# Gated linear attention in front of a token mixer: the attention rebuilt on 64-token blocks

## The chip, the core and the metric

The kernel runs on one core of one Trainium2 chip. The metric is the device time of one execution in microseconds, read as the median of several runs. The engines are named as in the profile: PE multiplies matrices (PEld loads its stationary side), DVE, ACT and POOL are the elementwise engines, and SP issues the DMA transfers.

## The reference

Four batches with eight heads of width 40 run over 768 tokens. Each head carries a 40x40 state C and a normalizer n; both fade by the forget gate and grow by the input gate, with a running maximum m that keeps the exponentials small:

```python
m_new  = np.maximum(f_gate[:, :, t] + m, i_gate[:, :, t])
f_stab = np.exp(f_gate[:, :, t] + m - m_new)
i_stab = np.exp(i_gate[:, :, t] - m_new)
C = f_stab * C + i_stab * outer(v_t, k_t);   n = f_stab * n + i_stab * k_t
h_t = sigmoid(o_gate_t) * (C @ q_t) / max(|n . q_t|, 1)
```

The heads are put side by side to rows x of width 320, and the mixer follows: theta = x @ w_theta, zr = x cos(theta), zi = x sin(theta), y = w_tok_r @ zr + w_tok_i @ zi over the tokens, u = x + y, and the output u + relu(u @ w_ch). The three weight matrices arrive as 64-bit floating point, handed over as integers, and the kernel turns each into a sum of two 32-bit parts; a mixer product is then three products of parts.

## The kernel before

The work is cut into 24 attention tasks, n = 4c + b for chunk c (six chunks of 128 tokens) and batch b, and 12 mixers, q = 2c + pr, one for two batches. A task loads q and k transposed (`qk`), and k and v by token (`tok`). The matrix E of decays, 128 x 8 x 128, comes in chunk 0 from four PE products (`assemble`, L292) and in the later chunks from a broadcast load of cumulated gates out of DRAM (L425), on which ACT takes an exponential with one bias per head (L430, eight a task). POOL clears what is not causal (L436). PE makes the scores `sc` from 64-row halves, two heads at a time (L445), DVE multiplies them by E (L449), and PE sums, per head, the scores times the values, into the single-bank tile `ph` (L464). Behind chunk 0 the state is read into the same sums: queries scaled by the decay (`qs`, L453) against C, three heads in one product of 120 rows (L461). From `ph` DVE takes the denominator (L474, L475), the output gate (L480) and the output X (L486). For the next chunk the keys are faded (L500), PE makes the state's growth `st` (L506), the old state is faded (`wane`, L510) and DVE adds the growth (`up`, L519). One state a chunk is carried, for 128 tokens.

A mixer transposes X (L542), splits it into two parts (L544, L545), makes the angles (L557, L563), rounds them to whole turns, takes sine and cosine on ACT (L582, L583), multiplies by X (`zm`, L588) and splits again (`zh`, `zl`, L589, L590). Five groups of twelve products (L601) mix the tokens of a chunk into all 768, and DVE adds each group to the accumulator `acc` (L616; for chunk 0, L608 to L612). The weights of a chunk come in two pieces, each turned into two parts by `split`: size (`_abs`), two exponent steps (`_up`, L343 and L344), sign (L347), low bits (L350), rounding (L358) and remainder (L359). At the end `channel` splits u and makes the channel products (L671, L681), DVE adds the relu (L691) and SP stores.

PSUM holds three tiles of two banks (`two`) and two of one bank (`one`). Nothing is scheduled at run time: every step is a task with the engines that may do it, and the string `ORDER` lists number and engine (T for PE, V, A, G, D for a DMA issue on SP) of each in the order of issue. Each engine works its part of this list in order; a tile's slot goes round in the same order.

Of the kernel before, what the change touches and what calls it, by code (L numbers as in the profile page):

```python
# [8 lines left out]
F32 = mybir.dt.float32  # L9
# [8 lines left out]
DM = H * D  # L18
# [4 lines left out]
KD = 3 * D  # L23
TOK = 9 * D + H * E1
# [4 lines left out]
HEAD = [3 * g + j for j in range(3) for g in range(3) if 3 * g + j < H]  # L29
RANK = [HEAD.index(h) for h in range(H)]  # L30
SPREAD = (0,)
# [4 lines left out]
LEAST = 2.0**-15  # L36
WCOLS = 1792

ORDER = """
4V 24T 0D 1D 2V 60V 62V 63V 3A 108D 67A 70D 61G 64V 68V 69G 65A 109V 82D 66V 71A 74D 83A 141D 124D 143T 145A 126T 111V  # L40
144A 84V 112V 148T 113V 72D 110G 131T 142D 125D 127A 114V 128A 75A 209T 147G 85V 116V 115D 129G 86V 73A 119T 208D 130G
132V 87A 146G 133V 150V 149V 76V 121V 88A 134T 77V 120A 151T 210A 78V 291D 89G 211A 192T 93A 135V 122A 152V 190D 79A
155G 136V 207D 153V 138G 101D 194A 213G 80A 193A 123D 293D 212G 214T 197T 195G 137V 102A 216V 154V 156T 157A 94D 158T
117T 196G 294D 139T 81G 215V 191D 199V 159A 118A 198V 217T 160V 295D 140V 95A 90A 161A 274D 103V 200T 92A 91A 218V
272D 162T 301G 297A 163T 104V 96V 105V 221G 296A 219V 276D 201V 202V 106A 275D 164A 204G 292D 220V 298G 360D 203V 165V
306G 299T 280T 300V 222T 356D 224T 278A 337D 277A 166V 273D 59G 282G 279G 362A 225V 223V 361A 226V 97V 167A 281V 302T
98V 227A 583D 168A 169V 402D 205T 228T 229T 364T 172V 341D 270D 170V 107G 357D 345T 303V 358D 99A 206A 230A 173A 171V
174V 271A 363G 231V 232V 283T 100G 365V 284V 285V 308G 187T 188V 304V 409D 233A 305V 289G 359D 234A 422D 418D 403A
287A 189V 178T 286V 235G 180V 410V 416D 307T 437D 343A 179V 184T 411V 366G 340D 186V 185V 238G 342A 412V 236A 309V
175T 367T 424A 239V 177V 338D 373A 344G 339D 176V 413V 346V 263D 368V 288T 414A 420D 310T 181T 311A 290V 369V 182V  # L50
312V 371G 347G 370V 441D 404V 419D 237V 348T 372T 352V 405V 183A 314T 423A 315T 354A 421D 442A 240G 313V 440D 406V
445T 439D 426T 374V 425G 415G 443A 316A 264A 317V 353T 444G 427V 244T 250T 355V 318A 446V 417A 428V 407A 433G 319A
349V 265V 320A 429T 253T 587D 350V 438D 351V 266V 267V 252A 268A 408G 246V 256D 324G 257A 245V 434T 255V 487D 435G
447G 436V 325A 483D 486D 430V 241T 488A 431V 251V 555D 448T 258V 489A 502D 259V 485D 321G 260V 247T 506D 254V 449V
452G 484D 242V 491T 450V 504D 248V 432V 322A 261A 454G 243A 510T 249V 490G 375T 451V 503D 507A 492V 376A 453T 505D
493G 508A 498V 262G 509G 455V 589A 648D 494T 377V 379T 326V 500G 499T 568D 588A 694D 495V 517G 511V 456T 380T 378V
381A 501V 269V 457A 496V 591T 512G 585D 323G 562D 382V 590G 383V 513T 564D 385A 458V 566D 556V 584D 695V 389G 331T
459V 384A 592V 386G 519V 586D 332V 569A 570A 565D 514V 563A 598G 515V 460T 652D 461T 516V 462A 572T 463V 327T 593G
328V 594T 390V 653A 497V 521T 567D 518T 571G 573V 574V 654A 391G 629D 464V 335T 524V 595V 466A 729D 522A 523V 333T
# [82 lines left out]


@with_exitstack
def mlstm_mixer(ctx: ExitStack, tc: tile.TileContext, gates, qk, q3, tok, og, wtok, wth, wch, table_d, out):
    nc = tc.nc
    plan = Plan()
    add = plan.add
# [54 lines left out]

    dma = nc.sync.dma_start


    gt = Tile(w_k)

    def cols(n):
# [609 lines left out]
```

## Time and profile before

| | us |
|---|---|
| median of three runs | 349.94 |
| runs | 349.14, 351.73, 349.94 |
| span of the profiled execution, first to last instruction | 347.3 |
| PE, DVE busy in that span | 309.7, 297.2 |
| ACT, POOL busy in that span | 187.0, 162.3 |

The profiled execution is one more run of the same program. Its record has a span and no time of its own; the runs have times. The span is 2.6 us below the median, which is what lies around the instructions. Busy times of PE are modelled, since its matmuls are pipelined; where the text needs a matmul's cost it takes the distance of starts.

### The profile page before, as it was taken

What the parts mean: (1) busy time and instruction counts of PE and PEld (TensorE: products, weight loads), DVE (VectorE), ACT (ScalarE), POOL (GpSimd) and SP (SyncE); (2) the same over time, 40 slices, a digit from 0 to 9 for tenths busy, and PEclk for the clock granted to TensorE, in tenths of its full rate; (3) what the DMA queues carried; (4) which work ended last, traced back from release to release, by engine and by line L of the source; (5) the groups of instructions that cost most, each with busy time, mean ns of one, the idle gap of its engine ahead of it and who ended that gap; (6) DMA issues with size and microseconds to landing.
All of it is one profiled execution on the core that took longest, in us unless ns stands there. A gap on an engine that the chain in (4) does not pass through costs nothing.

```text
span 347.3 us, 5976 instructions
## 1 busy us (share of the span) xinstructions
PE 309.7 (89%) x2246; PEld 295.6 (85%) x2246; DVE 297.2 (86%) x468; ACT 187.0 (54%) x375; POOL 162.3 (47%) x122
## 2 busy tenths in 40 slices
PE   1559886997999989898979999889999999999994
PEld 0559876987998979798979999889999999998994
DVE  2999999899999998999999969998999796897231
ACT  2857888937767688757539384649334221140000
POOL 0836675645486864531492258552128432644000
PEclk9969998799899989998999999999999999999999
DMA  4968999718469895096557775355301000001423
GB/s 145 346 215 285 327 366 318 271 32 295 162 205 303 262 295 196 9 286 215 165 178 278 259 262 156 98 144 174 116 3 45 2 0 0 2 0 47 161 113 136
DMA packets 20912, 59.66 MB, mean 172 GB/s; under 512 B 2191, under 2 KB 7700, under 8 KB 20884
## 3 DMA queue, kind: packets, MB, share of 16 engines
q1 hardware_dynamic: 20884, 59.28, 51.3%
q8 instruction: 18, 0.29, 0.3%
q14 instruction: 10, 0.08, 0.1%
HBM read 55.17 MB, written 4.10 MB: 171 GB/s over the span
## 4 chain that ended last, share of the span: by engine, by line
PE 54%; DVE 36%; DMA 4%; issue 3%; POOL 1%; ACT 0%; SPq 0%; DVEq 0%; POOLq 0%; ACTq 0%
PE two L601 28%; PE two L671 7%; PE one L464 5%; PE two L557 3%; DVE E L449 3%; PE two L445 3%; DVE val L347 3%; PE one L461 2%; DVE val L343 2%; DVE sg L480 2%; DMA w<-in_gates 2%; DVE val L344 2%; DVE z L590 2%; DVE C L527 2%; DMA tok<-in_tok 2%
## 5 line engine op out<-in xcount | busy, mean ns | idle before, releaser
L601 PE MATMUL two<-w,z 128*128 128x384 f32 x720 | 139.7, 350 | 8.2 <-DVE r L573 5.3
L601 PEld LDWEIGHTS two<-w,z 128*128 128x128 f32 x720 | 129.6, 196 | 10.9 <-DVE r L573 6.3
L616 DVE TENSOR_TENSOR acc<-two,acc 128x768 f32<-128x768 f32 x50 | 46.7, 949 | 8.7 <-PE two L601 8.5
L430 ACT ACTIVATE E<-E,biasT 128x128 f32<-128x128 f32 x160 | 49.4, 391 | 7.3 <-DMA E<-g_d 7.1
L436 POOL TENSOR_SCALAR_AFFINE_SELECT E<-E 128x1024 f32<-128x1024 f32 (+1 forms) x28 | 33.7, 1211 | 33.5 <-ACT E L430 30.9
L464 PE MATMUL one<-tok,E 128*128 128x41 f32 x320 | 42.7, 272 | 0.5 <-issue 0.4
L464 PEld LDWEIGHTS one<-tok,E 128*128 128x128 f32 x320 | 41.0, 193 | 0.9 <-DVE E L449 0.9
L449 DVE TENSOR_TENSOR E<-two,E 128x1024 f32<-128x1024 f32 (+1 forms) x28 | 29.4, 1060 | 2.0 <-POOL E L436 2.0
L461 PE MATMUL one<-C,q 120*128 120x123 f32 (+1 forms) x120 | 26.3, 301 | 2.9 <-DVE C L527 1.3
L671 PE MATMUL two<-u,w 128*128 128x384 f32 x156 | 28.5, 339 | 0.3 <-DVE acc L616 0.3
L445 PE MATMUL two<-qk 64*128 64x128 f32 x384 | 26.0, 285 | 2.8 <-DVE acc L550 1.5
L445 PEld LDWEIGHTS two<-qk 64*128 64x128 f32 x384 | 24.4, 196 | 4.6 <-DVE acc L616 1.8
L671 PEld LDWEIGHTS two<-u,w 128*128 128x128 f32 x156 | 26.8, 188 | 1.6 <-issue 1.0
L588 POOL TENSOR_TENSOR ab<-ab,X 128x640 f32<-128x640 f32 x10 | 16.3, 1631 | 19.5 <-ACT ab L583 19.5
L359 POOL TENSOR_TENSOR w<-val,w 128x768 fp32r<-128x768 f32 x9 | 18.4, 2043 | 13.8 <-ACT w L358 8.6
L691 DVE SCALAR_TENSOR_TENSOR acc<-two,acc 128x768 f32<-128x768 f32 x10 | 9.3, 954 | 17.2 <-PE two L681 9.3
L557 PE MATMUL two<-wth,xs 128*128 128x320 f32 x144 | 23.5, 312 | 0.5 <-DVE acc L550 0.5
L453 POOL TENSOR_TENSOR q<-q,eb 120x384 f32<-120x384 f32 x12 | 14.6, 1219 | 16.6 <-PE two L445 11.4
L557 PEld LDWEIGHTS two<-wth,xs 128*128 128x128 f32 x144 | 21.5, 188 | 0.9 <-issue 0.9
L461 PEld LDWEIGHTS one<-C,q 120*128 120x128 f32 x120 | 18.9, 192 | 4.0 <-issue 2.5
L590 POOL TENSOR_TENSOR z<-r,z 128x640 fp32r<-128x640 f32 x9 | 16.0, 1778 | 10.4 <-ACT z L589 5.3
L569 ACT ACTIVATE r<-two 128x640 f32<-128x640 f32 x11 | 7.7, 701 | 23.8 <-PE two L563 23.5
(120 smaller groups left out, 540.3 us busy)
## 6 DMA issues: line engine op xcount, KB each, us to landing
qk<-in_qk SPq DMA_DIRECT2D x24, 512.0 KB, 5.7
E<-g_d SPq DMA_DIRECT2D x20, 512.0 KB, 4.6
raw<-in_wtok SPq DMA_DIRECT2D x12, 768.0 KB, 7.0
tok<-in_tok SPq DMA_DIRECT2D x24, 344.0 KB, 6.5
out<-acc SPq DMA_DIRECT2D x10, 384.0 KB, 2.5
q<-in_q SPq DMA_DIRECT2D x20, 180.0 KB, 4.6
eb<-e_d SPq DMA_DIRECT2D x20, 180.0 KB
sg<-in_og SPq DMA_DIRECT2D x5, 640.0 KB, 7.7
```

Of the source, the lines that this page charges most:

```text
L359: add(name + "_lo", "GV", lambda e: ENG[e].tensor_sub(lo(), v(), hi().bitcast(F32)), [val, *rest], step)
L430: nc.scalar.activation(u.E.t[:, r], u.E.t[:, r], AF.Exp, bias=biasT[:, c, b * H + r:b * H + r + 1])
L436: nc.gpsimd.affine_select(d, d, pattern=[[0, k], [1, P]], compare_op=ALU.is_ge, fill=0.0, base=0, channel_multiplier=-1)
L445: nc.tensor.matmul(u.sc.t[:, f, hp], u.qk.t[rows, 1, hp], u.qk.t[rows, 0, hp], start=True, stop=True)
L449: add(f"wg{n}{a}", "V", lambda e, a=a, z=z: nc.vector.tensor_mul(u.E.t.rearrange("p (f k) t -> p f (k t)", f=2)[:, a:z], u.sc.t[:, a:z], u ...
L461: nc.tensor.matmul(u.ph.t[:, 3 * g * E1:h1 * E1], u.q3.t[:KD, g, :], C[b][:, 3 * g:h1, :].rearrange("p h e -> p (h e)"), start=True, stop= ...
L464: nc.tensor.matmul(u.ph.t[:, h * E1:(h + 1) * E1], u.E.t[:, RANK[h], :], u.tok.t[:, 9 * D + h * E1:9 * D + (h + 1) * E1], start=False, sto ...
L557: nc.tensor.matmul(th.t[:, b, :DM], xs.t[:, x, k], wt5[:, y, k], start=(i == l == 0), stop=False)
L590: add(f"zl{q}{s}", "GV", lambda e, s=s, src=src: ENG[e].tensor_sub(zv(1, s), src.t, zv(0, s).bitcast(F32)), [src, z], n + 1.5)
L601: nc.tensor.matmul(pm.t[:, t, :TH], z.t[:, x, s, j * P:(j + 1) * P], wv(c, y, s, t), start=(k == 0), stop=(k == 5))
L616: add(f"ga{q}{j}", "V", lambda e, j=j, pm=pm, av=av: nc.vector.tensor_add(av, pm.t[:, :, :TH], av), [pm], n + 2.6 + 0.3 * j, swap="acc")
L671: nc.tensor.matmul(pm[jj].t[:, t, :TH], wcv(x)[:, col:col + P], up[pr, k][:, y, ts], start=(i == l == 0), stop=(jj == 2 and i == 4 and l = ...
```

## The change

The attention of a task is rebuilt; the mixer's arithmetic is kept.

- A chunk of 128 tokens is two blocks of 64, and the state is carried from block to block: C has two buffers per batch, `cw0`, `up0` make the state behind the first block and `cw1`, `up1` the one behind the second. Decays between the blocks need no 128 x 128 matrix: E shrinks to 128 x 2 x 256.
- All four products of a task (`sc`, `st`, `it`, `ph`) are made of 16 matmuls with 64 rows and 64 stationary columns, each on its own quarter of the array; heads 4 to 7 have their two token blocks swapped in `tok`, so that the quarters in a row differ.
- All decays, the causal mask included, are summed in PSUM for every task by four matmuls (`dd`) from operands made once a chunk (`operands`) or once (`masks`, `places`), and one exponential reads them. The loads `dt`, `eb` and `q3`, their DRAM stores, the selection on POOL and the eight exponentials are gone.
- The state is read with unscaled queries into a tile of its own (`it`); `pa` scales the result by the decay and `hv` adds the inner part.
- `split` makes size and first exponent step in one activation with a scale, so that one shift is left on DVE.
- PSUM is four tiles of two banks, for everything. The output gates are loaded and activated per mixer, in 12 pieces.
- `ORDER` is new as a whole. Behind the last angle product it has 7 mixing groups (14 before). The engine letters give, among others: X on POOL in 10 of 24 tasks, `pa` on ACT in 2, state fading `cw` on POOL 29 and DVE 15 times, `zm` on DVE 20 and POOL 4 times (7 and 17 before), `zl` 14 and 10 (9 and 15), `zh` on ACT 19 times (12).

```diff
-    two = slots("two", 3, [2, 512], pool=ps)
-    one = slots("one", 2, [512], pool=ps)
+    two = slots("two", 4, [2, 512], pool=ps)
...
+    def masks(b):
+        add(f"mask{b}", "GV", lambda e: ENG[e].tensor_tensor(
+            M[:, b], T["sel"][:, 4 * b:4 * b + 4].unsqueeze(2).broadcast_to([P, 4, L]),
+            T["tri"].unsqueeze(1).broadcast_to([P, 4, L]), op=ALU.add), (), -9.0 + b)
...
-        def upper(e):
-            nc.vector.tensor_scalar_max(v(), v(), LEAST)
-            nc.vector.tensor_scalar(vi(), vi(), 3, 0x3FFFFFF8, op0=ALU.logical_shift_left, op1=ALU.bitwise_and)
+        add(name + "_abs", "A", lambda e: nc.scalar.activation(v(), words(1).bitcast(F32), AF.Abs, scale=LESS), [rawt, val], step)
+        add(name + "_up", "V", lambda e: nc.vector.tensor_scalar(vi(), vi(), 3, None, op0=ALU.logical_shift_left), [val], step)
...
+        def assemble(e):
+            o = lambda f: u.dd.t[:, f, :4 * L].rearrange("p (k t) -> p k t", t=L)
             for f in range(2):
+                nc.tensor.matmul(o(f), W(c)[:, f], M[:, b], start=True, stop=False)
             for f in range(2):
+                nc.tensor.matmul(o(f), place[:, 2 * b + f], Gm(c), start=False, stop=True)
+        add(f"dd{n}", "T", assemble, [u.dd, WG[c]], n - 0.5)
+        add(f"exp{n}", "A", lambda e: nc.scalar.activation(u.E.t, u.dd.t[:, :, :4 * L], AF.Exp), [u.dd, u.E], n - 0.5,
+            table="exp")
...
         def score(e):
             for k in range(4):
-                hp = slice(k * P, (k + 1) * P)
                 for f in range(2):
-                    rows = slice(64 * f, 64 * f + 64)
-                    nc.tensor.matmul(u.sc.t[:, f, hp], u.qk.t[rows, 1, hp], u.qk.t[rows, 0, hp], start=True, stop=True)
+                    for x in range(2):
+                        s = slice(L * x, L * x + L)
+                        nc.tensor.matmul(u.sc.t[half[x ^ f], f, k * L:(k + 1) * L], q4(1)[half[f], k, s],
+                                         q4(0)[half[f], k, s], start=True, stop=True)
...
         def state(e):
-            for g in range(3):
-                n1 = min(3, H - 3 * g) * E1
-                nc.tensor.matmul(u.st.t[:KD, 3 * g * E1:3 * g * E1 + n1], u.tok.t[:, g * KD:(g + 1) * KD],
-                                 u.tok.t[:, 9 * D + 3 * g * E1:9 * D + 3 * g * E1 + n1], start=True, stop=True)
+            for k in range(4):
+                for f in range(2):
+                    for x in range(2):
+                        r = half[x ^ f]
+                        h = 4 * f + k
+                        nc.tensor.matmul(u.st.t[half[f], x, k * E1:(k + 1) * E1], u.tok.t[r, h * D:h * D + L],
+                                         vt()[r, h], start=True, stop=True)
...
+        def carry(x):
+            f = wane[:, c, x, 4 * b:4 * b + 4].unsqueeze(2).broadcast_to([P, 4, E1])
+            add(f"cw{x}{n}", "GV", lambda e: ENG[e].tensor_mul(C[b][1 - x], C[b][x], f), (), n + 0.2)
+            add(f"up{x}{n}", "V", lambda e: nc.vector.tensor_add(C[b][1 - x], sv(x), C[b][1 - x]), [u.st], n + 0.3)
...
+        def inter(e):
+            for k in range(4):
+                for f in range(2):
+                    for x in range(2):
+                        s = slice(L * x, L * x + L)
+                        nc.tensor.matmul(u.it.t[half[x], f, k * E1:(k + 1) * E1], q4(0)[half[f], k, s], C[b][x][half[f], k],
+                                         start=True, stop=True)
...
+        def intra(e):
+            for k in range(4):
+                for f in range(2):
+                    for x in range(2):
+                        r = half[x ^ f]
+                        nc.tensor.matmul(u.ph.t[half[x], f, k * E1:(k + 1) * E1], u.E.t[r, f, k * L:(k + 1) * L],
+                                         vt()[r, 4 * f + k], start=True, stop=True)
...
+            nc.vector.tensor_mul(hv4(), v4(u.it), lt.rearrange("p (f k) -> p f k", f=2).unsqueeze(3).broadcast_to([P, 2, 4, E1]))
+        add(f"pa{n}", "VA", passed, [u.it, u.hv], n + 0.4)
+        add(f"hv{n}", "V", lambda e: nc.vector.tensor_add(hv4(), v4(u.ph), hv4()), [u.ph, u.hv], n + 0.5)
```

## Rows read from the trace of the kernel before

**Rows 1.** The page, part 1: busy us of each engine, share of the span, instructions.
```profile
PE 309.7 (89%) x2246; PEld 295.6 (85%) x2246; DVE 297.2 (86%) x468; ACT 187.0 (54%) x375; POOL 162.3 (47%) x122
```

**Rows 2.** Busy us (instructions) of each engine by stage, then PEclk, DMA share, GB/s.
```profile
0.00:59.60 59.60, 39.35 (x345) 35.90 (x345) 51.42 (x85) 42.48 (x77) 32.67 (x35) 0.93 0.83 286
59.60:140.00 80.40, 74.96 (x540) 71.51 (x541) 76.77 (x134) 58.14 (x122) 48.48 (x35) 0.93 0.69 223
140.00:229.00 89.00, 82.49 (x644) 79.39 (x642) 81.40 (x134) 55.02 (x122) 44.43 (x33) 0.98 0.57 186
229.00:279.40 50.40, 50.13 (x349) 48.98 (x349) 45.43 (x66) 22.19 (x37) 19.88 (x13) 1.00 0.26 83
279.40:347.30 67.90, 62.78 (x374) 59.84 (x372) 42.14 (x53) 9.18 (x18) 16.88 (x10) 1.00 0.15 59
```

**Rows 3.** The chain of waits in order of time: start us, us, what.
```profile
156.49 0.61 PE one L506 x6
...
281.83 23.25 PE two L601 x132
...
342.67 0.96 DVE acc L691
```

**Rows 4.** PE's instructions in order of time: start us, us, line, tile, shapes.
```profile
257.44 0.38 PE L461 MATMUL one<-C,q 120*128 120x123 f32 x2
...
259.81 2.00 PE L557 MATMUL two<-wth,xs 128*128 128x320 f32 x12
261.74 1.16 PE L445 MATMUL two<-qk 64*128 64x128 f32 x16
262.66 0.69 PE L563 MATMUL two<-wth,xs 64*128 64x320 f32 x6
...
278.73 0.71 PE L563 MATMUL two<-wth,xs 64*128 64x320 f32 x6
```

**Rows 5.** DVE groups by line and shape: xcount | busy us, mean ns | idle before.
```profile
L449 DVE TENSOR_TENSOR E<-two,E 128x1024 f32<-128x1024 f32 x20 | 24.2, 1212 | 1.9 <-POOL E L436 1.8
...
L480 DVE SCALAR_TENSOR_TENSOR sg<-den,sg 128x320 f32<-128x320 f32 x24 | 18.8, 790 | 0.4
...
L344 DVE TENSOR_SCALAR val<-val 128x768 int32<-128x768 int32 x12 | 12.1, 1005 | 0.4
...
L486 DVE TENSOR_TENSOR X<-one,sg 128x320 f32<-128x320 f32 x24 | 11.3, 482 | 0.4
...
L343 DVE TENSOR_SCALAR val<-val 128x768 f32<-128x768 f32 x12 | 9.5, 791 | 0.0
...
L527 DVE SCALAR_TENSOR_TENSOR C<-one,tab,C 120x123 f32<-120x123 f32 x32 | 9.3, 332 | 3.3 <-PE one L506 3.3
...
L590 DVE TENSOR_TENSOR z<-ab,z 128x640 fp32r<-128x640 f32 x6 | 6.9, 1154 | 0.0
...
L453 DVE TENSOR_TENSOR q<-q,eb 120x384 f32<-120x384 f32 x8 | 6.2, 774 | 0.0
...
L449 DVE TENSOR_TENSOR E<-two,E 128x512 f32<-128x512 f32 x8 | 5.1, 680 | 0.2 <-POOL E L436 0.2
...
L588 DVE TENSOR_TENSOR r<-r,X 128x640 f32<-128x640 f32 x5 | 4.1, 812 | 0.0
```

**Rows 6.** POOL groups by line and shape.
```profile
L436 POOL TENSOR_SCALAR_AFFINE_SELECT E<-E 128x1024 f32<-128x1024 f32 x20 | 26.9, 1347 | 30.9 <-ACT E L430 30.9
...
L588 POOL TENSOR_TENSOR r<-r,X 128x640 f32<-128x640 f32 x7 | 11.7, 1664 | 16.2 <-ACT r L582 16.2
```

**Rows 7.** Lines L480 and L616 alone: duration ns min/median/max, first and last start.
```profile
L480 DVE SCALAR_TENSOR_TENSOR sg<-den,sg x24: 439/560/1519, 29.6 to 271.2; 128x320 f32<-128x320 f32 x24
...
L616 DVE TENSOR_TENSOR acc<-two,acc x50: 907/948/959, 128.1 to 312.3; 128x768 f32<-128x768 f32 x50
```

**Rows 8.** ACT groups by line and shape.
```profile
L430 ACT ACTIVATE E<-E,biasT 128x128 f32<-128x128 f32 x160 | 49.4, 391 | 7.3 <-DMA E<-g_d 7.1
```

**Rows 9.** The page, part 6: DMA issues, KB each, us to landing.
```profile
E<-g_d SPq DMA_DIRECT2D x20, 512.0 KB, 4.6
```

More of the change, by code (lines that the diff above doesn't have):

```diff
@@ L22 @@
 R = B * H
-KD = 3 * D
-TOK = 9 * D + H * E1
+L = P // 2
+TOK = H * D + H * E1
+SU = S + L
 NT = B * DM // P
@@ L191, in mlstm_mixer @@
     ap = early.enter_context(tc.tile_pool(name="ap", bufs=1))
-    E_k = slots("E", 3, [H, P], pool=ap)
+    widths = (("tri", L), ("back", 2 * R), ("away", 2 * R), ("sel", B * 4), ("ends", 2 * B * 4),
+              ("place", 4 * B), ("keep", 4), ("side", P), ("head2", 2), ("minus", 1))
+    tab = ap.tile([P, sum(n for _, n in widths)], F32, name="tab")
+    T, at = {}, 0
+    for name, n in widths:
+        T[name] = tab[:, at:at + n]
+        at += n
+    place = ap.tile([P, 2 * B, P], F32R, name="placer")
+    M = ap.tile([P, B, 4, L], F32R, name="M")
+    hb = ap.tile([P, S + NC * L], F32R, name="hb")
+    leaveT = ap.tile([P, NC, R], F32, name="leaveT")
+    fadeT = ap.tile([P, NC, R], F32, name="fadeT")
+    wane = ap.tile([P, NC, 2, B * 4], F32, name="wane")
+    C = [[ap.tile([P, 4, E1], F32, name=f"C{b}{i}") for i in range(2)] for b in range(B)]
+    E_k = slots("E", 3, [2, 4 * L], pool=ap)
     qk_k = slots("qk", 3, [2, 4 * P], pool=ap)
     tok_k = slots("tok", 3, [TOK], pool=ap)
-    q3_k = slots("q3", 2, [3, P], pool=ap)
-    eb_k = slots("eb", 2, [3, P], pool=ap)
-    sg_k = slots("sg", 2, [B * DM], pool=ap)
-    den_k = slots("den", 3, [H, 1], pool=ap)
-    C = [ap.tile([KD, 9, E1], F32, name=f"C{b}") for b in range(B)]
+    sg_k = slots("sg", 3, [2 * DM], pool=ap)
+    den_k = slots("den", 2, [H, 1], pool=ap)
+    hv_k = slots("hv", 2, [H, E1], pool=ap)
+    wg_k = slots("wg", 2, [4, P], F32R, pool=ap)
     def load(name, fn, uses=(), step=0.0, after=()):
@@ L501, in attention @@
-        add(f"fade{n}", "GVA", fade, [u.tok], n + 0.4)
+            ENG[e].tensor_mul(kt(), kt(), f.unsqueeze(2).broadcast_to([P, H, D]))
+        add(f"fade{n}", "GVA", fade, [u.tok], n + 0.1)
+        u.st = Tile(two)
         def state(e):
-            for g in range(3):
-                n1 = min(3, H - 3 * g) * E1
-                nc.tensor.matmul(u.st.t[:KD, 3 * g * E1:3 * g * E1 + n1], u.tok.t[:, g * KD:(g + 1) * KD],
-                                 u.tok.t[:, 9 * D + 3 * g * E1:9 * D + 3 * g * E1 + n1], start=True, stop=True)
@@ L529, in attention @@
-        add(f"up{n}", "AV" if c == 0 else "V", grow, [u.st], n + 0.6)
-    done = {}
+            for k in range(4):
[5 more added lines that the diff above has]
+                                         vt()[r, h], start=True, stop=True)
+        add(f"st{n}", "T", state, [u.tok, u.st], n + 0.2, half=True)
@@ L591, in mixer @@
                 [src, z], n + 1.5)
+        mine = next(g for g in GROUPS[pr] if c in g)
+        if c != mine[-1]:
+            return
         for j in range(5):
@@ L735, in mlstm_mixer @@
             mixer(n // 2)
-    names = {f"X{n}" for n in range(NU - 4, NU)} | {f"ph{n}" for n in range(NU - 4, NU)} | {f"up{NU - 5}", f"wane{NU - 5}"}
+    names = {f"X{n}" for n in range(NU - 4, NU)}
     channel()
```

608 lines of the change are left out of this document (269 added, 339 removed).

## Prediction, made before the changed kernel ran

> **What bounds the kernel now.** I read the shares first [rows 1]: PE is busy for 309.7 us and DVE for 297.2 us of 347.3, the other two for half of it. An average over stages hides which of the two waits for the other, so the second view cuts the span where the work changes [rows 2]: the first mixing product starts at 59.6, and the last angle product ends at 279.4. Before that point DVE is busy for 51.4 + 76.8 + 81.4 + 45.4 = 255.0 us, 91.3% of the time, and PE for 39.4 + 75.0 + 82.5 + 50.1 = 246.9 us, 88.4%. Two engines that feed each other at these shares are both the bound: until 140 DVE is the fuller (96% of its second stage), from 229 on PE is (99%). Behind 279.4 PE alone sets the pace. The order of before leaves 14 mixing groups there, at 23.25 / 132 = 0.176 us a product [rows 3], so 12 x 0.176 = 2.11 us each and 29.6 us together; then 33.6 us of channel products and 4.6 us of last addition and store, 67.9 in all. The profiled span stands 2.6 us below the median of 349.94, and I add that to every span worked out below.
>
> **PE, part by part.** One task's attention products today: values and state read 257.44 to 259.81 = 2.37 us for 22 records, scores 261.74 to 262.66 = 0.92 us for 16 [rows 4], state update 0.61 us for 6 [rows 3]: 3.90 us for 44 records. What sets a record's time? The value records stream only 41 columns and still follow each other at 2.37 / 22 = 0.108 us, so it is the 128-column stationary side. Score records, 64 rows each, come two at a time: 0.92 / 8 pairs = 0.115 us a pair, nothing lost by sharing the array.
>
> The change issues 64 matmuls a task, 128 records in 32 fours, each a 64x64 quarter with a 64-column stationary side. No row shows a column half or a 64-column load, so I bound a four: 0.056 us if the load halves with its columns and all four overlap, 0.11 if one of the two fails, 0.22 if both do. That is 1.8, 3.5 or 7.1 us. Four array-mode entries at about 0.1 us (the score's 0.92 against 8 x 0.11) and four assembling matmuls of 256 columns (12 of 320 columns take 1.93 us [rows 4], so 0.13 each) add 0.4 + 0.5. A task then costs 2.7, 4.4 or 8.0 us; times 24, PE's work moves by -29, +13 or +98 us. I take the low end, because its nearest row, the paired scores, overlaps fully, and keep the others as rivals.
>
> One place speaks against the low end. The scores of before write their two row halves into two banks; state and value products of the change send both row halves into the same bank, in different partitions. The Trainium skill (TensorEngine Tiling (Array Packing), Restrictions and Gotchas) says that different row tiles cannot access the same PSUM bank simultaneously. By that rule the forecast below would become rival 2; no run here shows it.
>
> **DVE, part by part** (durations from [rows 5], counts from the engine letters of the new order). Gone or smaller: the decay product 29.3 us (24.2 + 5.1), now 24 x 0.68 = 16.3, as only half the columns are left: -13.0. One of the two size steps in 15 weight pieces, at about 0.8 (0.79 and 1.0): -12. Size on DVE in 4 pieces and three roundings, now ScalarE's: -6. Query scaling: -6.2. Ten of the 24 output products, now on POOL: 10 x 0.48 = -4.8. Seven roundings of z at 0.8 and five first copies into the accumulator at 0.95, both to ScalarE: -10.4. One fade and smaller moves: -7. New: 22 scalings of the state read and 24 additions, 328 columns from PSUM at about 0.49 (0.48 for 320): +22.5. State updates: some 66 instructions at about 0.3 become 44 + 15 of 164 columns at 0.36 (between 0.33 for 123 and 0.48 for 320): +1. Thirteen products with X at 0.81 and five remainders of z at 1.15 come over from POOL: +16.3. The gate chain gets about as many passes as it had: 0, at most 3 either way. Sum: -59.4 + 39.8 = -19.6, DVE's total 278.
>
> POOL loses the causal selection (26.9 us and smaller ones [rows 6]), query scaling, state fading and most of the products with X (1.66 each), and gets 29 small state products and ten outputs: 162 to about 105 us. That matters for DVE. An operation with both inputs in SBUF spreads widely (the output gate 439 / 560 / 1519 ns), one that reads PSUM doesn't (the accumulation 907 / 948 / 959) [rows 7]; both engines reach into SBUF, and the spread is the collision. The gate's mean of 790 ns against its least costs 24 x 0.35 = 8.4 us, and four or five groups of that kind exist, say 40 us. A third less POOL gives back some 13; the moved products are exposed in turn, so I take 6, with 0 and 13 as its ends.
>
> ScalarE loses 160 exponentials, 49.4 us [rows 8], for 24 of 512 columns, and gets fading in ten tasks and more of the weights; it stays near 187 us, 54%, and I cost it at nothing while it runs ahead of DVE. Without that cover its exponential, some 0.6 us, would head every task: 24 x 0.6 = 14 us. The broadcast loads of decays leave the DMA queue (20 x 512 KB [rows 9] and two kinds of 180 KB): 18 MB fewer, and 56 issues fewer on SP, where the second gate load now stands behind two weight loads; only the tasks from the fifth on need it. DMA is 83% busy in the first stage only [rows 2], so this buys calm there; I count 0, at best 3.
>
> **The sum.** The new order leaves seven mixing groups, not 14, behind the last angle product: 14.8 + 33.6 + 4.6, and 1 us where the last z is late: 54 us instead of 67.9. DVE does some 33 us of its work there, so 278 - 33 - 6 = 239 lie ahead. At the share that DVE keeps today, 239 / 0.913 = 262. PE would have 246.9 + 14.8 (the seven groups) - 29 = 233 us in these 262, 89%, as now: the two stay in balance. 262 + 54 + 2.6 = 318. What is late next is DVE again: scaling, addition, denominator, gate, product now follow each other, and PE's transposes wait for the last. A state read waits for DVE's first update, and behind it in PE's queue stand the value products and the mixing groups that would otherwise fill.
>
> **Rivals.** (1) *Quarters at half pace*: one overlap or the shorter load fails. PE has 246.9 + 14.8 + 13 = 275 us ahead of the tail; at the 95% that it holds when it is the bound (between 88 and 99%) 289, so 289 + 54 + 2.6 = 346, no change. For: no row shows a column half. Against: row halves overlap without loss. A rule of the Trainium skill would give the same end (TensorE: Matmul & The Clock Gate, under "Wait — 56ns, not 53.3ns?"): start-to-start never drops below about 25 ns, which makes 3.2 us of 128 records; the paired rows are too slow to test it.
> (2) *Two of the four groups at half pace*, because row halves that end in one bank take turns: 0.9 us a task, 24 x 0.9 = 21 us more of PE, 254 us at 93% of 273: 330. For: today's paired groups all write two banks, so no row excludes it. Against: the halves write different partitions.
> (3) *Quarters one after another* (0.22 a four): 246.9 + 14.8 + 98 = 360 us of PE, at 97% 371: 427.
> (4) *PSUM slots*, the slower side: before had three double slots and two single ones; now four double ones serve everything. Ahead of the tail 5 x 24 + 2 x 12 + 53 = 197 tiles pass through them, so each may be held 4 x 262 / 197 = 5.3 us (before: 3 x 279.4 / 98 = 8.6 for the double ones). A mixing group holds its slot for 2.1 + 0.95 us and its waits, and the state's tile until its second update, several DVE instructions later. From a mean hold of 5.3 us on PE waits for slots in order, with everything queued behind; at 6.0 us it is 295 + 56.6 = 352. Against: today's slots turn over fast enough with 91% DVE.
> (5) *More comes back*: contention gives its upper end and DVE's share rises to 94%: 232 / 0.94 + 56.6 = 303.
>
> **How the numbers follow.** Forecast 318 (308 to 328): 0.52; rival 5: 0.09; rival 2: 0.06; rival 1: 0.12; rival 4: 0.14; rival 3: 0.07. Runs of before differ by 0.7%, so 1% is about what a comparison can tell. Faster by over 1% (below 346.4): 0.52 + 0.09 + 0.06 + half of rival 1 = 0.73; within 1%: the other half and a third of rival 4, 0.11; slower: 0.16. The range from 300 to 354 takes in rivals 1, 2 and 5 and the price of rival 4, and leaves out about 0.16: rival 3, slots held much longer than 6 us, and a little below 300.
>
> **What would show it.** Right: score, state, read and value records in fours a few ns apart, each group of 32 in 0.45 to 0.6 us; DVE's total near 278 and the spread of the output gate smaller; POOL near 105; 54 us from the last angle product to the end. Wrong: groups of 0.9 us or more; PE waiting with DVE's PSUM readers as the releasers (rival 4); DVE's share ahead of the tail below 90%, which would mean that the longer chain of an output, and not the amount of work, sets the pace.

## The result, and the profile after

The changed kernel takes 321.34 us, median of 4 runs (320.37 to 321.89), against 349.54 for the kernel before measured beside it (4 runs, 348.48 to 351.73). The ratio is 0.918, interval 0.913 to 0.923: faster by 8.2%. The forecast was 318, range 300 to 354. The medians and ranges below are over all runs of a kernel; the ratios leave out the runs that lie more than 1.5% above its shortest. Line numbers below are those of the changed kernel where a row is from it. The texts written before each run say TensorE, VectorE, ScalarE and GpSimd for PE, DVE, ACT and POOL.

Part 1 of the page after (busy us, share of the span of 320.1, instructions), and from part 3 the queue that loads instructions:

```profile
PE 288.7 (90%) x4436; PEld 266.0 (83%) x4436; DVE 256.7 (80%) x462; ACT 185.7 (58%) x344; POOL 95.1 (30%) x100
...
q8 instruction: 35, 0.57, 0.8%
```

Beside [rows 1]: PE 21 us less, DVE 40 less, POOL 67 less, ScalarE as before. The same cuts as [rows 2], at the first mixing product (now 52.6) and the end of the last angle product (now 267.45):

```profile
0.00:52.60 52.60, 35.74 (x656) 28.35 (x657) 38.46 (x79) 35.56 (x79) 10.50 (x18) 0.68 0.64 219
52.60:140.00 87.40, 84.71 (x1400) 79.32 (x1399) 78.08 (x155) 61.32 (x109) 27.82 (x34) 1.00 0.42 140
140.00:229.00 89.00, 85.28 (x1420) 79.11 (x1419) 76.46 (x139) 60.68 (x114) 30.04 (x30) 0.98 0.41 138
229.00:267.45 38.45, 35.86 (x679) 33.68 (x677) 33.33 (x57) 17.02 (x23) 12.76 (x11) 1.00 0.14 43
267.45:320.10 52.65, 47.15 (x290) 45.53 (x288) 30.39 (x36) 11.17 (x22) 13.97 (x8) 0.98 0.19 75
```

Two things are to be seen. The span fell by 27.2 us: 279.4 - 267.45 = 12.0 ahead of the tail (the stretch behind the last angle product), and 67.9 - 52.65 = 15.3 in it. And the fuller engine is another: from 52.6 to 267.45 PE is busy for 97, 96 and 93% of the stages, DVE for 89, 86 and 87%. Before, DVE was the fuller engine in the first two stages.

PE's timeline shows a part of the products of a pair of tasks, with the assembling products (L412, L414), states (L445), scores (L424), values (L470) and state reads (L461); columns as in [rows 4]. Each of the 16 matmuls of a group has two records, so a whole group is x32:

```profile
247.96 0.51 PE L412 MATMUL two<-M,wg 128*128 128x256 f32 x2
248.30 0.40 PE L414 MATMUL two<-wg,placer 128*128 128x256 f32 x2
248.63 0.68 PE L445 MATMUL two<-tok 64*64 64x41 f32 x32
249.12 0.67 PE L424 MATMUL two<-qk 64*64 64x64 f32 x32
249.61 0.63 PE L445 MATMUL two<-tok 64*64 64x41 f32 x32
250.05 0.65 PE L470 MATMUL two<-tok,E 64*64 64x41 f32 x32
250.52 1.10 PE L461 MATMUL two<-C,qk 64*64 64x41 f32 x58
253.05 0.26 PE L461 MATMUL two<-C,qk 64*64 64x41 f32 x3 [1.43 <-issue]
```

Read the starts: a group of 32 quarter records follows the last in 0.44 to 0.49 us. The last line is something else: PE stood for 1.43 us and waited for nothing that the profile shows.

The line of the output gate and that of the accumulation alone (ns, min/median/max), which answer to [rows 7]:

```profile
L491 DVE SCALAR_TENSOR_TENSOR sg<-den,sg x24: 440/485/903, 32.1 to 260.0; 128x320 f32<-128x320 f32 x24
...
L597 DVE TENSOR_TENSOR acc<-two,acc x50: 907/950/959, 97.6 to 286.5; 128x768 f32<-128x768 f32 x50
```

The gate's longest falls from 1519 to 903 and its median from 560 to 485, while the operation that reads PSUM keeps its 907 to 959. Groups of DVE by line and shape, as in [rows 5]:

```profile
L427 DVE TENSOR_TENSOR E<-two,E 128x512 f32<-128x512 f32 x24 | 16.3, 680 | 0.0
L453 DVE TENSOR_TENSOR C<-two,C 128x164 f32<-128x164 f32 x44 | 13.8, 321 | 3.6 <-ACT r L539 2.9 <-PE two L445 0.4
...
L484 DVE TENSOR_TENSOR hv<-two,hv 128x328 f32<-128x328 f32 x24 | 11.9, 496 | 2.8 <-PE two L470 2.0
L491 DVE SCALAR_TENSOR_TENSOR sg<-den,sg 128x320 f32<-128x320 f32 x24 | 11.8, 513 | 0.2
...
L482 DVE TENSOR_TENSOR hv<-two,leaveT 128x328 f32<-128x328 f32 x22 | 10.9, 494 | 5.1 <-PE two L461 5.0
...
L560 DVE TENSOR_TENSOR z<-ab,z 128x640 fp32r<-128x640 f32 x7 | 5.8, 825 | 0.0
```

### The profile page after: what moved, and what is told of

Its sections match the earlier page's. It is cut to its first block, busy times and chain, and to the rows that moved or that the text cites. A ratio compares the mean times of both kernels' runs of the same rounds, so it can differ in the third digit from the quotient of the medians.

```text
span 320.1 us, 10207 instructions
## 1 busy us (share of the span) xinstructions
PE 288.7 (90%) x4436; PEld 266.0 (83%) x4436; DVE 256.7 (80%) x462; ACT 185.7 (58%) x344; POOL 95.1 (30%) x100
## 4 chain that ended last, share of the span: by engine, by line
PE 67%; DVE 17%; ACT 6%; issue 4%; DMA 3%; POOL 2%; DVEq 0%; POOLq 0%; ACTq 0%
PE two L574 31%; PE two L651 9%; PE two L527 6%; PE two L470 4%; PE two L461 3%; DMA w<-in_gates 3%; PE two L445 3%; PE two L424 3%; PE two L511 2%; PE two L533 2%; PE two L412 2%; DVE val L345 2%; PE two L661 2%; DVE xs L514 1%; PE two L414 1%
## 5 line engine op out<-in xcount | busy, mean ns | idle before, releaser
L597 DVE TENSOR_TENSOR acc<-two,acc 128x768 f32<-128x768 f32 x50 | 46.6, 949 | 8.2 <-PE two L574 8.1
L351 POOL TENSOR_TENSOR w<-val,w 128x768 fp32r<-128x768 f32 (+2 forms) x13 | 23.3, 1794 | 41.1 <-ACT w L350 40.8
L452 POOL TENSOR_TENSOR C<-C,wane 128x164 f32<-128x164 f32 x29 | 14.5, 508 | 37.3 <-PE two L461 35.6
L461 PE MATMUL two<-C,qk 64*64 64x41 f32 x768 | 18.7, 238 | 5.2 <-issue 2.3
L461 PEld LDWEIGHTS two<-C,qk 64*64 64x64 f32 x768 | 16.0, 145 | 7.9 <-issue 3.8
L445 PE MATMUL two<-tok 64*64 64x41 f32 x768 | 17.2, 237 | 4.8 <-ACT tok L433 2.5
L445 PEld LDWEIGHTS two<-tok 64*64 64x64 f32 x768 | 14.8, 144 | 7.2 <-ACT tok L433 2.8
L433 ACT ACTIVATE tok<-tok,fadeT 128x40 f32<-128x40 f32 x80 | 18.6, 317 | 3.4 <-DMA tok<-in_tok 3.4
L539 ACT ACTIVATE r<-two 128x640 f32<-128x640 f32 x12 | 8.5, 705 | 19.6 <-PE two L533 17.8
L424 PE MATMUL two<-qk 64*64 64x64 f32 x768 | 18.5, 235 | 1.0 <-issue 0.9
L470 PE MATMUL two<-tok,E 64*64 64x41 f32 x768 | 17.5, 238 | 1.7 <-issue 1.6
L424 PEld LDWEIGHTS two<-qk 64*64 64x64 f32 x768 | 15.4, 145 | 2.6 <-issue 1.9
```

Of the source, the lines that this page charges most:

```text
L351: add(name + "_lo", "GV", lambda e: ENG[e].tensor_sub(lo(), o(), hi().bitcast(F32)), [val, *rest], step)
L424: nc.tensor.matmul(u.sc.t[half[x ^ f], f, k * L:(k + 1) * L], q4(1)[half[f], k, s], q4(0)[half[f], k, s], start=True, stop=True)
L433: nc.scalar.mul(kt()[:, h], kt()[:, h], f[:, h:h + 1])
L445: nc.tensor.matmul(u.st.t[half[f], x, k * E1:(k + 1) * E1], u.tok.t[r, h * D:h * D + L], vt()[r, h], start=True, stop=True)
L452: add(f"cw{x}{n}", "GV", lambda e: ENG[e].tensor_mul(C[b][1 - x], C[b][x], f), (), n + 0.2)
L461: nc.tensor.matmul(u.it.t[half[x], f, k * E1:(k + 1) * E1], q4(0)[half[f], k, s], C[b][x][half[f], k], start=True, stop=True)
```

## The experiments

Times of runs that were not made together are compared through the kernel before, which ran in each (medians 348.85 to 350.22). Twelve kernels ran.

### Which engine sets the pace after the change

**Less DVE work in the changed kernel** (leaves out denominator and output gate, so the result lacks the division and the gate). The same edit was made to the kernel before, below.

```diff
-        add(f"den{n}", "V", den, [u.hv, u.den], n + 0.5)
+        add(f"den{n}", "V", lambda e: None, [u.hv, u.den], n + 0.5)
...
-        add(f"og{n}", "V", lambda e: nc.vector.scalar_tensor_tensor(
-            s3(), u.den.t.broadcast_to([P, H, D]), 1.0, s3(), op0=ALU.min, op1=ALU.mult), [u.den, sg[n // 2]], n + 0.5)
+        add(f"og{n}", "V", lambda e: None, [u.den, sg[n // 2]], n + 0.5)
```

> The changed kernel without the denominators (left out: the absolute value, the reciprocal and their product with the output gate): DVE loses 24 x (0.207 + 0.203 + 0.513) = 22 us, and each task's chain about 1 us. If DVE's work sets the pace at the share on record, the time falls by 18 to 24 us. If PE sets it, by 0 to 6 us.

317.29 us (315.48 to 318.56), ratio 0.909 [0.9015, 0.9165]. DVE's busy time fell from 256.7 to 239.1, and 4 us came of it. Even these need not be DVE's: PE's busy time fell by 5.3 us with no product left out, at a granted clock of 0.951 against 0.937.

```profile
PE 283.4 (90%) x4436; PEld 262.1 (84%) x4436; DVE 239.1 (76%) x390; ACT 185.3 (59%) x344; POOL 95.4 (30%) x100
```

**More PE work in the changed kernel, few instructions** (half of 20 mixing groups computed a second time into the same place).

```diff
-                for t in range(2):
+                for t in ((0, 0, 1) if pr and 0 < cc < 5 else (0, 1)):
```

> The changed kernel with the first half of 20 mixing groups computed a second time into the same place (120 products more, 21 us of TensorE in few instructions, none for another engine). Theory 'TensorE sets the pace after': it passes on all of it, 321 + 19 to 23, so 340 to 344 us, and the stalls of TensorE without any wait (5.7 us in the profile of after) stay as they are, since few instructions are added. Theory 'VectorE at 85% and the waits between the two set it': about a half, 328 to 334.

344.27 us (343.28 to 346.24), ratio 0.9858 [0.9803, 0.9914]: 23 us more for 23.5 us more of PE's busy time. The second part of the expectation was missed: the stands without a wait grew from 4.8 us to 7.6.

```profile
PE 312.2 (91%) x4556; PEld 290.4 (84%) x4556; DVE 256.7 (75%) x462; ACT 185.9 (54%) x344; POOL 94.5 (27%) x100
```

So after the change PE's work is passed on whole and DVE's at a fifth at most. PE sets the pace.

**Score products twice in the changed kernel** (same PSUM place, same result).

```diff
-            for k in range(4):
+            for k in (0, 1, 2, 3, 0, 1, 2, 3):
```

> Every task of the changed kernel makes its scores twice into the same tile: PE gets 24 x 0.49 = 11.8 us of work that nobody waits for in particular, DVE nothing. If DVE's work sets the pace ahead of the tail (the prediction's account), PE has room and the time rises by 0 to 4 us. If PE sets it (the rival that the trace of after suggests, with PE busy for 93 to 97% between 52.6 and 267), it rises by 9 to 13 us.

340.9 us (334.55, 340.04, 341.75, 343.39), with 11.3 us more of PE's busy time: 300.0 against 288.7. The shortest run is 13.2 us above the change, which is little more than PE's work and near the 9 to 13 expected. The other three are 19 to 22 above it. The profile is of the longest, and its timeline shows where more time went:

```profile
200.99 1.16 PE L424 MATMUL two<-qk 64*64 64x64 f32 x64
201.97 0.51 PE L470 MATMUL two<-tok,E 64*64 64x41 f32 x21
205.16 0.37 PE L470 MATMUL two<-tok,E 64*64 64x41 f32 x10 [2.68 <-issue]
```

PE's idle time of this kind is 4.8 us in the changed kernel and 17.0 in this run; what the shortest run had of it is not known. This led to the runs on instruction loading below.

### What set the pace before

**Score products twice in the kernel before** (same edit in its score loop).

```diff
-            for k in range(4):
+            for k in (0, 1, 2, 3, 0, 1, 2, 3):
```

> The kernel before with its scores made twice into the same tile: PE gets 24 x 0.92 = 22 us, DVE nothing. If DVE alone set the pace before, 0 to 8 us more; if PE and DVE were both the bound, as the prediction read it, 10 to 18 us; if PE alone, 19 to 24 us.

354.77 us (350.29 to 355.56), ratio 1.0125 [1.0009, 1.0241]: 4 to 5 us for 14.5 more of PE's busy time, at a granted clock of 0.981 where the kernel before had 0.966.

```profile
PE 324.2 (92%) x2630; PEld 312.7 (88%) x2630; DVE 296.3 (84%) x468; ACT 187.4 (53%) x375; POOL 161.4 (46%) x122
```

**Less DVE work in the kernel before** (denominator and gate left out).

```diff
-        add(f"den{n}", "V", den, [u.ph, u.den], n + 0.3)
+        add(f"den{n}", "V", lambda e: None, [u.ph, u.den], n + 0.3)
...
-        add(f"og{n}", "V", out_gate, [u.den, sg[c]], n + 0.3)
+        add(f"og{n}", "V", lambda e: None, [u.den, sg[c]], n + 0.3)
```

> The kernel before without the denominators (left out: the absolute value, the reciprocal and their product with the output gate): DVE loses 18.8 + 8.5 = 27 us. If DVE alone set the pace before, the time falls by 22 to 30 us; if both were the bound, by 8 to 18 us; if PE alone, by 0 to 6 us.

346.37 us (343.08 to 349.7, 10 runs), ratio 0.9897 [0.9853, 0.9941]: 3.6 us for 19.6 less of DVE. (The instructions left out had 27; in this trace, that of the longest run, the rest of DVE's work took longer.)

```profile
PE 310.5 (89%) x2246; PEld 298.0 (86%) x2246; DVE 277.6 (80%) x396; ACT 187.3 (54%) x375; POOL 159.1 (46%) x122
```

By the ranges named for them, the first of these two runs says that DVE alone set the pace, and the second that PE alone did. They can't both be so, and neither run shows what was expected of two engines that are both the bound.

**Less PE work in the kernel before** (a third of the part products of 30 mixing groups left out of the result).

```diff
-                        for x, y in parts:
+                        for x, y in parts[:2 if less else 3]:
```

> The kernel before, with the third of the three part products left out of 30 of its 60 mixing groups (120 products of 0.176 us by the chain's row of 132 in 23.25 us, so TensorE has 21 us less; the result lacks that part). This is the amount by which the change cut TensorE's busy time. Theory 'TensorE was the pace before as it is after': 349 - 15 to - 21, so 328 to 334 us. Theory 'VectorE was the pace before', as the prediction had it: the products were beside its work, so at most 4 us go, 345 to 349. Theory 'before, the two engines waited for each other in turn, and neither alone is the pace' (taking 27 us from VectorE alone gave 3.3 us): 5 to 12 us go, 337 to 344.

350.37 us (346.51 to 352.02, 10 runs), ratio 1.003 [0.9987, 1.0073]: nothing. Two of the three theories expected 5 us or more. The time fits the other, DVE as the pace, and against that one stands the run without the denominators: 27 us of DVE's instructions less gave 3.6. Its page and the end of its last angle product (279.61 + 0.71, against 279.4 in [rows 2]):

```profile
PE 297.0 (85%) x2126; PEld 278.9 (80%) x2126; DVE 299.9 (86%) x468; ACT 187.2 (54%) x375; POOL 159.8 (46%) x122
```
```profile
279.61 0.71 PE L563 MATMUL two<-wth,xs 64*128 64x320 f32 x6
```

Of the 21 us of products, PE's busy time lost 12.7. The clock tells of a part of the rest: in its stage from 140 to 229 the granted clock was 0.92, where [rows 2] have 0.98.

**Both left out of the kernel before** (the two edits above).

> The same 120 products left out and the 48 denominator and output gate operations of VectorE left out as well (each alone: the run beside this one, and 346.4 us). Theory 'they waited for each other in turn': together they give clearly more than the two gains added, 349 - 20 to - 28, so 321 to 329 us. Theory 'one engine is the pace, the other's work lies beside it': the gains add, that of the products alone and 3 us more.

340.27 us (337.58 to 342.19), ratio 0.9745 [0.9664, 0.9827]: 2.5% less, where the two alone add to 0.7%. Its page and its last angle product:

```profile
PE 292.1 (87%) x2126; PEld 275.9 (82%) x2126; DVE 278.0 (83%) x396; ACT 187.0 (56%) x375; POOL 159.8 (47%) x122
```
```profile
268.43 0.71 PE L563 MATMUL two<-wth,xs 64*128 64x320 f32 x6
```

It ends at 269.1, near the 267.45 of the change, and the tail is 336.5 - 269.1 = 67.4, as before. That is what two engines that wait for each other in turn would show: taken from either one alone, some 20 us gave 0 to 4, and from both together 9. They brought the stretch ahead of the tail near the length that it has after the change, where it holds seven mixing groups more. That the two are the whole of it is not shown, as the next run tells. The sum of 20 to 28 us that this theory expected was too high: in the order of before, nothing of it reaches the tail.

**No causal selection in the kernel before** (28 instructions of GpSimd left out, the mask is missing from the result).

```diff
-            add(f"sel{n}{f}", "G", select, [u.E], n - 0.3)
+            add(f"sel{n}{f}", "G", lambda e: None, [u.E], n - 0.3)
```

> The kernel before without the causal selections of GpSimd (28 instructions, 33 us; the scores' mask is left out, so the result is not the reference's). Theory 'the selections lengthen VectorE's instructions when they run beside them': the output gate of 439 to 1519 ns (mean 790) falls below 650 and the sum of VectorE's busy time falls by 8 us or more, with no instruction of VectorE left out. Theory 'contention was worth 6 us in all, as the prediction had it': less than 4 us. Time: as taking 27 us of VectorE away gave 3.3 us, 344 to 349 by the theory of the two engines waiting in turn; 335 to 341 if the chain from ScalarE over GpSimd to VectorE was the pace.

340.22 us (335.75 to 345.94), ratio 0.9728 [0.9559, 0.9897]; the interval is wide, and the profile is of the longest run. DVE's busy time fell from 297.2 to 288.2 with none of its instructions gone, so the selections beside it cost DVE some 9 us (the two runs above in which DVE's work is unchanged have 296.3 and 299.9). The page, and the gate, to be read against [rows 5] and [rows 7]:

```profile
PE 310.0 (90%) x2246; PEld 297.7 (87%) x2246; DVE 288.2 (84%) x468; ACT 187.1 (54%) x375; POOL 127.8 (37%) x94
```
```profile
L480 DVE SCALAR_TENSOR_TENSOR sg<-den,sg 128x320 f32<-128x320 f32 x24 | 16.1, 678 | 0.4
```
```profile
L480 DVE SCALAR_TENSOR_TENSOR sg<-den,sg x24: 439/491/1505, 28.0 to 268.2; 128x320 f32<-128x320 f32 x24
```

The mean of 678 stayed above the 650 named, as some gates still run beside other work of GpSimd, but the sum is beyond the 8 us named. The time lies in the range named for the chain from ScalarE over GpSimd to VectorE (335 to 341), and not in that of the two engines in turn (344 to 349). GpSimd's selections, of an engine that was busy for 47% of the span, were worth as much (2.7%) as the work taken from both fuller engines together (2.5%). The 9 us of DVE don't explain it, as 19.6 us less gave 3.6. So what set the pace before is not told by PE and DVE alone. That it was the chain is not shown either: in the trace of the kernel before, DVE waits for selections for 2.0 us in all.

### What the quarters are worth

**Score quarters in a row** (the same 16 products, 32 records, ordered by quarter; timed in 2 runs).

```diff
-            for k in range(4):
-                for f in range(2):
-                    for x in range(2):
+            for f in range(2):
+                for x in range(2):
+                    for k in range(4):
```

> The changed kernel with the 32 quarter products of each score task issued by quarter, eight of one quarter in a row, instead of one of each quarter in turn. Same products, same number of instructions. Theory 'quarters on different parts of the array run beside each other' (the prediction's term, 0.49 us for 32 records in the profile of after): in a row on one part each takes about 0.06 us, 1.9 us a task, so 24 x 1.4 = 34 us more of TensorE, and as TensorE sets the pace nearly all of it shows: 345 to 357 us. Theory 'they are short because they have 64 columns, and run one behind the other anyway': 0.5 us a task as before, 321.

331.97 us (331.61 and 332.33), ratio 0.9534 [0.9362, 0.9706]. PE has 307.0 us, 18.3 more.

```profile
148.29 1.36 PE L424 MATMUL two<-qk 64*64 64x64 f32 x29
...
149.50 0.22 PE L424 MATMUL two<-qk 64*64 64x64 f32 x1
```

A group of 32 takes about 1.25 us instead of 0.49: 0.039 us a record in a row, 0.015 in turn. Quarters do run beside each other, by a factor of 2.5 against the row order, where I expected 4. The time rose by 10.6 us only; in this run PE's stands without a wait fell to 2.2 us, which is a part of the difference, and the rest is not traced.

### PE's stands without a wait

**Mixing groups moved into the four runs of quarter groups** (five groups moved in the order, three of them with their additions; the first group of the ninth mixer is shown).

```diff
-881A 911V 825T 882V
+881A 911V 882V
...
-947T 885A
+947T 825T 885A
```

> The changed kernel with five mixing groups moved in the order of the tasks, into the four runs of six to nine quarter groups in which TensorE stood 1.1 to 1.8 us without waiting for a semaphore, each time 1 us after an instruction fetch had begun. Theory 'the fetch of the next 256 instructions doesn't keep up with a run of quarter groups': with a mixing group of 2 us in each run the four gaps of 5.7 us go, and as TensorE sets the pace the time falls by 3 to 6 us, to 315 to 318. Theory 'the gaps lie beside waits anyway, or the fetch costs the same wherever it falls': no change within 1 us, 321, or gaps elsewhere.

325.98 us (324.71 to 327.46), ratio 0.933 [0.9281, 0.9378]: slower by 4.6, though all the stands are gone. (The 5.7 us of the expectation counts from start to start, the 4.8 above counts idle time.) The starts of the transposes (L511) against those of the change tell where. At 80.12 this run is 1.8 us behind (78.30), long before a group was moved; its granted clock from 54 to 60 us was 0.73 there and 1.00 in the change. At 220.99 it is 1.5 behind (219.49), at 245.62 it is 3.1 (242.49), and at 266.38 it is 4.2 (262.19). The moves at 232 and at 251 us thus cost 1.6 and 1.1. PE's timeline from 230 on:

```profile
231.37 2.34 PE L574 MATMUL two<-w,z 128*128 128x384 f32 x12 [0.68 <-DVE acc L597]
233.64 0.69 PE L424 MATMUL two<-qk 64*64 64x64 f32 x32
234.76 0.68 PE L461 MATMUL two<-C,qk 64*64 64x41 f32 x32 [0.43 <-DVE acc L597]
...
241.69 4.09 PE L574 MATMUL two<-w,z 128*128 128x384 f32 x22 [0.61 <-DVE z L560]
```

The moved mixing groups wait for a PSUM place that DVE's accumulation (L597) frees, and so does what stands behind them. In place of a stand of 0.9 us there are three waits of 1.7 together.

**Only the moves at 188 and 232 us** (three of the five).

```diff
-798V 787G
+798V 680T 787G
...
-800T 680T 806G
+800T 806G
```

> The changed kernel with only three of the five moves of the run with all four runs broken up: the mixing groups put into the runs at 188 and 232 us. The two others (before the run at 152, and the last state, score and output products at 251 us) stay as in the changed kernel. In that run the stretch of the first of these two moves kept pace with after, that of the second gained 2 us, the move at 152 lost 1 and the one at 251 lost 4, as the last pair's products came later. Theory 'the fetch stall is worth its gap where the moved group delays nothing that others wait for': 321.3 - 1.5 to - 3, so 318 to 320 us, gaps near 188 and 232 gone, those near 153 and 251 there. Theory 'moving a group costs as much as the gap': 321 to 323. Theory 'the slower time had other causes than the move at 251 us': 324 to 327.

321.27 us (319.19 to 325.3, 7 runs), ratio 0.9137 [0.9064, 0.9211], where the change has 0.918: no difference that can be told. The gains and losses by move in this expectation (and so the blame on 251 us) came from starts of transposes that I had paired wrongly; those above are the right ones. PE's longest idle times by the view of waits from 50 to 265 us, first of the change and then of this run:

```profile
PE two L461 <- issue: 2.3, 2, 1.4
PE two L470 <- issue: 1.6, 1, 1.6
PE two L574 <- DVE acc L587: 1.2, 2, 1.0
...
PE two L424 <- issue: 0.9, 1, 0.9
```
```profile
PE two L461 <- issue: 2.2, 2, 1.4
PE two L574 <- DVE z L560: 1.4, 2, 0.7
...
PE two L470 <- DVE acc L597: 1.1, 1, 1.1
PE two L574 <- DVE acc L597: 1.0, 2, 0.7
```

2.6 us of stands went, and waits for DVE's accumulation (L597), 2.1 us together, came in their place. The move at 188 us alone did pay: between the transposes at 177.38 and 198.07 lie 20.7 us, in the change 21.8 (179.28 to 201.04). The move at 232 gave it back: 216.50 to 241.16 is 24.7 us, in the change 23.0. As a whole, moving the groups cost as much as the gaps. No version that I ran beats the change.

### The cold start

**Four warm-up groups more in the first stage** (they are defined in the kernel, only the order changes).

```diff
-4V 53T 54T 60G
+4V 53T 54T 55T 56T 57T 60G
...
-107A 173T 157T 132V
+107A 173T 157T 58T 132V
```

> The changed kernel with four of the eight-product warm-up groups that it already defines but doesn't issue placed in the first stage: three behind the last one issued, one behind the first state product. In the profile of after TensorE stands from 7.7 to 13.1 us and then works at a granted clock of 0.50 until 41 us, with 3.6 us for the angle products that take 1.9 later. Theory 'TensorE is the pace from its first work on': if the clock stays up, the first mixing group starts 4 to 10 us earlier than 52.6 and the time falls by as much, to 311 to 317. Theory 'the first stage is set by VectorE, ScalarE and the loads': the clock rises and nothing else does, 320 to 322. Loss if the groups hold up the first real products: up to 5 us, 326.

330.59 us (327.55 to 331.36), ratio 0.9502 [0.9381, 0.9622]: 9 us slower, beyond every end that I gave. The window from 20 to 40 us of this run, then that of the change:

```profile
20.00:40.00 20.00, 15.13 (x312) 11.79 (x315) 19.11 (x40) 18.50 (x41) 5.09 (x6) 0.87 0.63 203
```
```profile
20.00:40.00 20.00, 14.88 (x256) 13.67 (x257) 18.82 (x37) 17.41 (x37) 4.40 (x6) 0.50 0.63 203
```

The clock rose from 0.50 to 0.87, and the second transposes came 2.3 us earlier (55.50 for 57.79). The third came 2.1 us later (80.43 for 78.30), for which this run's timeline has the lines:

```profile
75.73 0.55 PE L470 MATMUL two<-tok,E 64*64 64x41 f32 x20 [2.37 <-issue]
76.20 3.92 PE L574 MATMUL two<-w,z 128*128 128x384 f32 x12
```

A stand without a wait, and behind it a mixing group of 3.92 us instead of 2.35: the granted clock from 74 to 82 us was 0.79, in the change 1.00. With four warm-up groups more in PE's queue the instruction loads fall at other places of the work, and all such stands of this run add to 10.4 us, 5.6 more than in the change. That fits the profiled loss of 5.7 (325.8 for 320.1) with the 2.3 us of the start spent on the slower clock; the parts were not tried one by one.

## Why the prediction was right, point by point

**The quarters: right.** Two assembling products of each kind take 0.67 us and four groups 0.44 to 0.49: 2.6 us a task, forecast 2.7. State and value groups, whose row halves end in one bank, are as short as score groups: 0.49 and 0.47. By the Trainium skill (TensorEngine Tiling (Array Packing), Restrictions and Gotchas) different row tiles cannot access one PSUM bank simultaneously, so they would have had to take turns; the trace disagrees for this pattern, and rival 2 falls. Rival 1 falls with it. The rule of the Trainium skill that would have led to it (TensorE: Matmul & The Clock Gate, "Wait — 56ns, not 53.3ns?") has starts never less than about 25 ns apart; the trace disagrees for four quarters in turn, where 32 records in 0.49 us are 15 ns each. Rival 3 had 0.22 us a four; the groups have 0.49 / 8 = 0.06, and even with quarters in a row a four takes 0.16. One term was read wrongly: the score's 0.92 us against 8 x 0.11 leaves 0.04 us for an array-mode entry, not 0.1, and the measured groups leave no more than that over eight fours of 0.056.

**PE's total: -29 forecast, -21 measured.** The terms by task hold at full clock, but two things of the first stage were put at nothing. The order of the changed kernel issues 16 warm-up products at its start, the one of before two; first the row of the change, then that of before:

```profile
1.45 6.28 PE L244 MATMUL two<-ones 128*128 128x512 bf16 x16 [1.45 <-DVE w L229]
```
```profile
1.52 1.04 PE L233 MATMUL two<-ones 128*128 128x512 bf16 x2 [1.52 <-DVE w L223]
```

That is 5.2 us more of PE's busy time, at a place where PE has nothing else to do: its next product starts at 13.13. And from 20 to 40 us, where 14.9 us of its busy time lie, PE's granted clock was 0.50, the lower of its two levels. At the other level that work would take about half, by an estimate from the twelve large angle products, which take 3.5 us there and 1.84 at 245 us. The two are more than the 8 us that are missing; what stands against them is not separated.

**The tail: right.** 54 us forecast, 52.65 measured, from seven mixing groups instead of 14. More than half of the fall of the span stands here, and the run with both edits shows that less work alone doesn't give it: its tail is 67.4. But the seven groups are not gone; they stand ahead of the tail now, in room that the quarters made. Counted by engine, 21.0 of the 27.2 us are busy time of PE and 6.2 are its idle time. No run has the new products in the order of before, so what each is worth alone is not shown.

**DVE: count right, contention mis-sized.** Most single operations came out near their terms (680 ns, 321, 494 and 496 against 680, 360, 490 and 490); the output X, which now has both inputs in SBUF, takes 677 ns on DVE, where it took 482 with one in PSUM [rows 5]. The total was to be 278 - 6 = 272 and is 256.7. The term of 6 us for contention (0 to 13) was too small: the selections alone cost some 9 in the kernel before, and the output gate, 24 x (790 - 513), gives 6.6 by itself. The two steps of `split` for sign and low bits, 24 instructions of the same kind and size as before, give 5.3 more (28.9 us before, 23.6 after). GpSimd ended at 95 us, forecast 105. The further terms of the 15 us are not separated.

**The failed step: "at the share that DVE keeps today, 239 / 0.913 = 262".** DVE has 226.3 us ahead of the tail, not 239, and at 91.3% that would be 248. The stretch took 267.45, because the ruler was the wrong engine: PE, at 241.6 us (233 forecast) and 90.3%, sets the pace there. A DVE term 13 us too high, and a share that no longer ruled, came out 5 us from the truth together: that the forecast lies so near is luck in this step. The test that the prediction named (DVE below 90%) came true, but not for the cause that it gave: it isn't the longer chain of an output, as 23.5 us more of PE pass on 23 and PE waits little for DVE in the view of waits above. For the kernel before, "the two are both the bound" holds so far as relief of one alone is worth little, but it left out a third: the selections on GpSimd, which the prediction counted only as contention, were worth as much as relief of both. The 2.6 us added to every span is a small error beside this: time less span of one and the same run is 1.7 to 2.1 us in all runs on record, and 2.6 came from the span of one run and the median of others.

**Rival 4, PSUM slots: no.** The largest of PE's waits on DVE between 50 and 265 us adds up to 1.2 us. **Rival 5: half.** Contention did give back more than its share, but what was freed on DVE could not be had while PE set the pace.

## What to carry to other kernels

Where two engines stand near 90% and take turns, cutting one may show nothing: try both at once before judging either, try the half-busy engine that feeds them as well, and ask which of them will rule after the change, since the share of one is no ruler for a kernel that the other paces. Price the order separately from the work: here the order took seven groups out of the tail, into room that the cheaper products had made, and what each gave alone was not tried. When matmuls become many and short, count instructions too.

## What the runs showed of the hardware

**Loading instructions can hold up PE.** 24 tasks of 128 quarter records doubled the loads on the instruction queue (18 of them in the kernel before, 35 after, 16 KB each by 0.57 MB / 35). In runs of six to nine quarter groups PE stands for 0.9 to 1.6 us, and up to 2.7 with the scores twice; each of the four stands of the changed kernel began a little over 1 us after such a load had begun. The DMA view of the stretch from 249 to 256 us, in which PE stood from 251.6 to 253.05, has one at about 250.4 and a second at about 254, when PE had gone on:

```profile
q8 instruction: 2, 0.03, 2.5%
```

The Trainium skill (Runtime: NRT & Kernel Launch, Instruction fetch mechanics) has these loads mostly hidden; here they are, where mixing products stand between, and are not in the runs. Breaking up the runs removed every stand, and with quarters in a row, the same instructions at a slower pace, 2.2 us of 4.8 are left. That shows the place. That it is the load itself that PE waits for is inferred from the times, and the stands of 7.6 us in the run with more mixing products, which adds few instructions, are not explained.

A long stand can cost twice, as the mixing group of 3.92 us behind one of 2.37 shows. The changed kernel has such a place too. Behind its stand of 1.58 us, which ended at 190.20, the granted clock was 0.71 until 196, and two mixing groups took 5.85 us from start to start, where the two behind the stand of 0.91 us took 4.29 at a granted clock of 1.00:

```profile
190.56 6.01 PE L574 MATMUL two<-w,z 128*128 128x384 f32 x24
```

**Quarters of the array overlap by more than a pair does**: 0.015 us a record across four quarters, 0.039 with one quarter at a time for eight records, a factor of 2.5. The pair has 0.058 (0.92 us for 16 scores) beside 0.108 for the value records of the whole array, both from [rows 4], a factor of 1.9.

**PE's clock partly undoes what is done to PE's work.** Products taken out (21 us) left 12.7 us less of busy time, and a granted clock of 0.941 to 0.973 over ten runs, mean 0.954, where the kernel before had a mean of 0.969 beside them. Scores twice (22 us) gave 14.5 us more, and 0.981 to 0.995 over four runs, where it had a mean of 0.965.
